# A recurrent-memory attention kernel with a dense branch: two more dense tiles put off into the steps, another layout of what is put off, and K's first matmul set moved into Q's group

## The chip, the cores and the metric

The kernel runs on one core of one Trainium2 chip. The metric is the device time of one execution in microseconds (us). Its engines here: PE (TensorE, matmuls; its weight loads are listed as PEld), DVE (VectorE), ACT (ScalarE), POOL (GpSimd) and SP (SyncE, which here only issues transfers). Each takes its instructions in the order in which the program gives them.

## The reference

Two branches read the same x (2048 tokens of 512), and a gate mixes them. Branch A goes over the tokens in 64 segments of 32. Each segment is put behind a memory of 8 rows, all 40 rows go through a 32-head attention, and the first 8 rows of its output are the memory of the next segment: the 64 steps must be done one after the other. Branch B is a layer norm and a two-layer network with GELU, and has no such chain.

```python
g = _sigmoid((x * gate_w).sum(-1, keepdims=True))
# branch A, for s in range(64), mem = mem0 at first
h = concatenate([mem, x[:, 32*s:32*s+32]], axis=1)          # 40 rows
q, k, v = (einsum('btd,dhe->bhte', h, W) for W in (Wq, Wk, Wv))
p = softmax(where(mask, einsum('bhqe,bhke->bhqk', q, k) * scale, -1e9))
o = einsum('bhte,hed->btd', einsum('bhqk,bhke->bhqe', p, v), Wo)
mem = o[:, :8];  outs.append(o[:, 8:])
# branch B
b = gelu(layernorm(x) @ w1 + b1) @ w2 + b2                  # 512 -> 1376 -> 512
return g * a + (1 - g) * b
```

## The kernel before

All instructions are in an order written out by hand, and each engine keeps to it.

**The front.** Branch B comes first, while the weights of branch A are loaded. It goes over 8 blocks of two tiles of 128 tokens. For each block there are 11 units, one for each 128 rows of the hidden layer: `a_mm` makes four matmuls of 256 columns (first layer, both tiles) and a Gelu on ACT into `hTm`; two units later `b_mm` makes one matmul of 512 columns for each tile of the block that is not in `DEF` (second layer, L487), and `ct_out` evicts the finished tile and stores it in DRAM (`c_dr`). The tiles in `DEF`, (1, 3, 5, 9, 11, 13, 15), are put off: `spill` (L501) stores their hidden layer in DRAM (`h_dr`) on SP's queue, 6 units in one transfer and 5 in a second. SP's queue also has the loads of x (`ld_x`), of the weights Wv, Wq, Wk, Wo (`loads`, L320 and L323, in this order) and the transposed loads `load_xT` (L102), all in program order. After the blocks come two `b_mm` that are left and `first()`, which makes the first tile's left-over Q, K and V.

**The hand-off.** The steps' tiles take memory that the front used. POOL clears the two `UT` tiles there (L615) once the front's users are through, and then copies into `QT` (`prep_q`, L249), which the first step's scores need.

**The steps.** Four steps, si = 0 to 3, share one tile of 128 tokens; `T` is the tile's number. A step holds 8 memory rows and 24 of its 32 tokens; the other 8 tokens of the four steps are done together, as fill, a tile ahead or behind (`side`, `run`). PE's order in a step: Q and K in four groups of four `qk_unit` (one for each chunk kc of the 512 inputs; each is four matmuls of 512 columns, side by side in the array's columns, called a set below), then scores, V, the sums for the softmax, attention times V (`av`), the output projection (`wo_pass`, eight sets), and `new_mem`, which makes the next memory, transposed, in three parts: ACT casts `w` (L741), PE gathers rows with `SelM` (L750), and DVE copies them into chunk 0, chunk 1 and chunks 2 and 3 of the next step's `hT` (L752). The next step's first `qk_unit` needs chunk 0, its second chunk 1, and so on.

**The put-off tiles in the steps.** `mlp` yields half sets: four matmuls of 256 columns into bank `W` (L678), 22 for a tile, and after the last of a tile `mlp_out` (L669) evicts W on DVE and stores the tile. From step 1 on a step has two such slots, `next(mlp, None)`, one ahead of `msum(1)` and one ahead of `recip_x`; tile 0's step si = 2 and the last tile's first steps have more. `recip_x` loads as many hidden-layer pieces `hm` as were used up (`hm_load`), between the store of R and the load of Rb on SP's queue.

**Banks.** The accumulators are U[0] to U[3], X1, X2, SbF and W. The four Q and K groups go to U[0] to U[3] in order; `out_sel` of tile T - 2 uses U[2] at si = 0, ahead of new_mem, which uses U[0], U[1] and a part of SbF.

Of the kernel before, what the change touches and what calls it, by code (L numbers as in the profile page):

```python
# [10 lines left out]
BF16 = mybir.dt.bfloat16  # L11
I32 = mybir.dt.int32
ACTF = mybir.ActivationFunctionType
ALU = mybir.AluOpType
# [14 lines left out]
def kernel(ctx, tc, A_x, A_mem0, A_Wq, A_Wk, A_Wv, A_Wo, A_seg_len, B_x, B_w1, B_b1, B_w2, B_b2, gate_w, out):  # L29
    nc = tc.nc  # L30
    P = 128
    _, S, Dm = A_x.shape
    H, Dh = A_Wq.shape[1], A_Wq.shape[2]
    M = A_mem0.shape[1]
# [4 lines left out]
    KC = Dm // P  # L39
    NT = S // P  # L40
    SPT = P // seg
    FC = (F + P - 1) // P
# [9 lines left out]
    scale = float(Dh) ** -0.5  # L52
# [5 lines left out]
    dram = ctx.enter_context(tc.tile_pool(name="dram", bufs=1, space=DRAM))  # L58
# [6 lines left out]
    omg = pers.tile([P, NT], FP32)  # L65
    w2_sb = pers.tile([P, FC, Dm], BF16)
    c_dr = dram.tile([S, Dm], BF16, name="c_dr")
    DEF = (1, 3, 5, 9, 11, 13, 15)
    h_dr = {T: dram.tile([FC, P, P], BF16, name=f"h_dr{T}") for T in DEF}
    r_dr = [dram.tile([P, NG], FP32, name=f"r_dr{i}") for i in range(2)]  # L70


# [17 lines left out]
    FR = F - (FC - 1) * P  # L90
# [20 lines left out]
    U = [lps.tile([P, 512], FP32, name=f"U{i}") for i in range(4)]  # L111
# [13 lines left out]
    def qk_unit(bk, G, t, hf, kc):  # L125
        h0, h1 = HF[hf]
        for j in range(4):
            nc.tensor.matmul(bk[32 * j:32 * j + 32, :], lhsT=G[:, kc, :], rhs=W5[t][:, kc, h0:h1, j, :],  # L128
                             start=(kc == 0), stop=(kc == KC - 1), tile_position=(0, 32 * j))
# [171 lines left out]
    with tc.tile_pool(name="mlpw", bufs=1) as mlpw, \  # L301
         tc.tile_pool(name="mwork", bufs=2) as mwork, \
         tc.tile_pool(name="msmall", bufs=2) as msmall:
        TB = 2
# [103 lines left out]


        for i in range(2):  # L410
            nc.gpsimd.memset(hTm[i][FR:P, FC - 1, :], 1.0)
        z_all = mlpw.tile([P, NT], FP32)
        th = mlpw.tile([P, NT], FP32)

# [57 lines left out]
        def bp(blk, tt):  # L472
            return U[2 * (blk % 2) + tt]

        def a_mm(blk, fc):
            rows = min(P, F - fc * P)
            n = blk * FC + fc
            hp = (SbF, W, U[3], SbF)[n] if n < 4 else (W, SbF)[n % 2]
            for kc in range(KC):
                nc.tensor.matmul(hp[:rows, 0:TB * P], lhsT=w1_sb[:, kc, fc * P:fc * P + rows], rhs=yTs[blk][:, kc, :], start=(kc == 0), stop=(kc == KC - 1))  # L480
            nc.scalar.activation(out=hTm[blk % 2][:rows, fc, :], in_=hp[:rows, 0:TB * P], func=ACTF.Gelu_apprx_tanh, bias=b1_sb[:rows, fc:fc + 1], scale=1.0)

        def b_mm(blk, fc):
            rows = min(P, F - fc * P + 1)
            tts = [tt for tt in range(TB) if blk * TB + tt not in DEF]
            for tt in tts:
                nc.tensor.matmul(bp(blk, tt)[:], lhsT=hTm[blk % 2][:rows, fc, tt * P:(tt + 1) * P],  # L487
                                 rhs=w2_sb[:rows, fc, :], start=(fc == 0), stop=(fc == FC - 1))
            if fc == FC - 1:
                for tt in tts:  # L490
                    if tt == 0 or blk == NBLK - 1:
                        ct_out(blk, tt)
                    else:
                        late.append(lambda: ct_out(blk, 1))

        def spill(blk, a, b):
            for tt in range(TB):
                T = blk * TB + tt
                if T in DEF:
                    src = hTm[blk % 2][:, :, tt * P:(tt + 1) * P]  # L500
                    nc.sync.dma_start(h_dr[T][a:b].rearrange("f p t -> p f t"), src[:, a:b])  # L501

        late = []

        def ct_out(blk, tt):
            T = blk * TB + tt
            ct = mwork.tile([P, Dm], BF16, tag="ct", bufs=4, name="ct")
            if blk < NBLK - 1:
                nc.scalar.activation(out=ct[:], in_=bp(blk, tt)[:], func=ACTF.Copy, scale=omg[:, T:T + 1])
            else:  # L510
                nc.vector.tensor_scalar(out=ct[:], in0=bp(blk, tt)[:], scalar1=omg[:, T:T + 1], scalar2=None, op0=ALU.mult)
            (nc.gpsimd if blk < NBLK - 1 else nc.sync).dma_start(c_dr[T * P:(T + 1) * P, :], ct[:])

        def first_h():
            m0p = X1[:].bitcast(BF16)[:, 0:KC * M].rearrange("p (k m) -> p k m", k=KC)
# [31 lines left out]
        for n, (blk, fc) in enumerate(units):  # L547
            a_mm(blk, fc)
            if n == len(units) - 1:
                dummy = msmall.tile([P, 1], FP32, tag="dummy", name="dummy")  # L550
                nc.scalar.activation(out=dummy[:], in_=omg[:, 0:1], func=ACTF.Exp)
            while late:
                late.pop(0)()
            if n >= LAG:
                b_mm(*units[n - LAG])
            if fc == 0:
                if blk >= 1:
                    gates(blk - 1)
                if blk + 1 < NBLK:
                    prep(blk + 1)  # L560
                else:
                    gate_sums(blk)
                    for _ in consts():
                        pass
            if blk + 1 < NBLK:
# [58 lines left out]
    def run(n):  # L624
        for _ in range(n):
            next(fill, None)
# [25 lines left out]
    def hm_load(n):  # L652
        for _ in range(n):
            if work:
                T, fc = work.pop(0)
                hm = cw.tile([P, P], BF16, tag="hm", bufs=5, name="hm")
                nc.sync.dma_start(hm[:], h_dr[T][fc])
                hms.append((T, fc, hm, 1))

    def hm_load4():  # L660
        x = cw.tile([P, Dm], BF16, tag="c", name="c").rearrange("p (k t) -> p k t", k=KC)
        T, fc = work[0]
        nc.sync.dma_start(x[:], h_dr[T][fc:fc + KC].rearrange("f p t -> p f t"))
        for k in range(KC):
            hms.append((*work.pop(0), x[:, k], 0))

# [74 lines left out]
            nc.scalar.copy(out=w[:, a:b], in_=bk[:, a:b])  # L741
        return w

    def new_mem(w, hn, n):

        k0, nk = ((0, 1), (1, 1), (2, 2))[n]
        bk = (U[0][:, 0:M], U[1][:, 0:M], xs8z)[n]
        for k in range(nk):
            for c in range(4):
                nc.tensor.matmul(bk[32 * c:32 * c + 32, M * k:M * k + M], lhsT=w[:, (k0 + k) * P + 32 * c:(k0 + k) * P + 32 * c + 32], rhs=SelM[:],  # L750
                                 start=n < 2, stop=True, skip_group_check=True, tile_position=(0, 32 * c))
        nc.vector.tensor_copy(out=hn[:, k0:k0 + nk, RIDE:32], in_=bk.rearrange("p (k m) -> p k m", k=nk))  # L752


    WS = ((2, 2, 1), (2, 2, 2), (2, 2, 2), (2, 2, 2))
    for s in range(nseg):
        T, si = divmod(s, SPT)
# [16 lines left out]
            load_xT(T + 2)  # L774
        if s in (2, (NT - 1) * SPT):
            hm_load4()
        for n, (t, hf) in enumerate(((0, 0), (1, 0), (0, 1), (1, 1))):
            bk = U[n]
            for kc in range(KC):
                qk_unit(bk, hc, t, hf, kc)  # L780
            if n == 0:
                flush(act_q, 9)
                flush(dve_q, 9)
            qk_tr(qk_cast(bk[:]), (QT, KT)[t], hf, LEFT * (1 - t))
            if n == 0:
                mask_put(1)
# [68 lines left out]
        new_mem(w, hn, 1)  # L855
        run(1)
        new_mem(w, hn, 2)
        for _ in fill:
            pass
        if si == 3 and T + 2 < NT:  # L860
# [197 lines left out]
```

## Time and profile before

| | us |
|---|---|
| median of 3 runs | 759.55 |
| lowest and highest | 757.79, 761.52 |
| the profiled execution | 759.91 |
| its span | 758.1 |
| busy: PE, ACT, DVE, POOL | 741.6, 537.3, 398.5, 274.8 |
| TensorE clock granted, mean | 0.999 |

The span is from the first to the last instruction of the profiled execution; its own time has some 1.8 us around it. Busy times are unions, so that matmuls that overlap count once. A matmul's record has a modelled end, with a tail behind its streaming: what a set costs is read from the distance of starts.

### The profile page before, as it was taken

What the parts mean: (1) busy time and instruction counts of PE and PEld (TensorE: products, weight loads), DVE (VectorE), ACT (ScalarE), POOL (GpSimd) and SP (SyncE); (2) the same over time, 40 slices, a digit from 0 to 9 for tenths busy, and PEclk for the clock granted to TensorE, in tenths of its full rate; (3) what the DMA queues carried; (4) which work ended last, traced back from release to release, by engine and by line L of the source; (5) the groups of instructions that cost most, each with busy time, mean ns of one, the idle gap of its engine ahead of it and who ended that gap; (6) DMA issues with size and microseconds to landing.
All of it is one profiled execution on the core that took longest, in us unless ns stands there. A gap on an engine that the chain in (4) does not pass through costs nothing.

```text
span 758.1 us, 45047 instructions
## 1 busy us (share of the span) xinstructions
PE 741.6 (98%) x19742; PEld 423.4 (56%) x19742; DVE 398.5 (53%) x1414; ACT 537.3 (71%) x1628; POOL 274.8 (36%) x517
## 2 busy tenths in 40 slices
PE   8999999999999999999999999999999999999997
PEld 5776455555555555555555556555555555555554
DVE  5767544545455545446454545445454545455454
ACT  5667677777777777777777777776777777677764
POOL 4001234433344343344333443434443344333441
PEclk9999999999999999999999999999999999999999
DMA  9999523222222323222222213231222212222222
GB/s 294 333 309 334 154 74 63 68 85 77 72 66 67 91 67 94 66 82 60 82 78 75 85 36 99 67 83 57 76 77 84 82 56 74 66 87 70 62 81 61
DMA packets 74971, 75.70 MB, mean 100 GB/s; under 512 B 42505, under 2 KB 64882, under 8 KB 73234
## 3 DMA queue, kind: packets, MB, share of 16 engines
q1 hardware_dynamic: 73730, 71.07, 30.7%
q8 instruction: 156, 2.56, 1.4%
q0 software_dynamic: 496, 1.18, 0.7%
q10 hardware_dynamic: 544, 0.52, 0.2%
q14 instruction: 45, 0.37, 0.2%
HBM read 59.49 MB, written 6.98 MB: 88 GB/s over the span
## 4 chain that ended last, share of the span: by engine, by line
PE 86%; issue 1%; ACT 0%; DVE 0%; DMA 0%; POOL 0%; DVEq 0%
PE U L128 33%; PE X L159 18%; PE X L147 17%; PE X L128 4%; PE U L290 3%; PE W L678 2%; PE U L147 2%; PE U L266 1%; PE U L750 1%; PE SbF L266 1%; PE SbF L705 1%; PE U L295 1%; PE U L277 1%; PE U L280 0%; PE U L270 0%
## 5 line engine op out<-in xcount | busy, mean ns | idle before, releaser
L734 POOL TENSOR_TENSOR UT<-XR,Rb 128x384 bf16<-128x384 bf16 x126 | 140.3, 1136 | 309.0 <-DMA Rb<-r_dr 237.8
L133 ACT CAST Tb<-U 128x512 bf16<-128x512 f32 x288 | 168.7, 586 | 81.8 <-PE U L128 78.9
L128 PEld LDWEIGHTS <-hT 128*32 128x32 bf16 x4096 | 107.6, 96 | 100.5 <-DVE hT L752 8.1
L147 PE MATMUL X<-Wv_sb,hT 128*32 128x512 bf16 x2048 | 144.6, 378 | 0.3 <-issue 0.2
L128 PE MATMUL U<-Wq_sb,hT 128*32 128x512 bf16 x2048 | 136.5, 381 | 0.2 <-DVE hT L752 0.2
L128 PE MATMUL U<-Wk_sb,hT 128*32 128x512 bf16 x2048 | 133.1, 379 | 0.0
L159 PE MATMUL X<-Wo_sb,UT 128*32 128x512 bf16 x2016 | 121.1, 380 | 0.0
L752 DVE CAST hT<-U 128x8 bf16<-128x8 f32 x126 | 20.9, 166 | 166.1 <-PE U L750 126.0
L812 ACT CAST V<-X 128x256 bf16<-128x256 f32 x256 | 88.7, 372 | 15.9 <-PE X L147 3.3
L137 DVE STREAM_TRANSPOSE QT<-Tb 128x256 f32<-128x256 f32 x128 | 56.6, 442 | 73.3 <-ACT Tb L133 72.5
L159 PEld LDWEIGHTS <-UT 128*32 128x32 bf16 x2048 | 56.4, 96 | 54.8 <-issue 14.3
L711 ACT CAST XR<-U 128x256 bf16<-128x256 f32 x252 | 78.5, 436 | 0.0
L741 ACT CAST w<-X 128x128 bf16<-128x128 f32 x189 | 44.8, 310 | 44.9 <-PE X L159 44.9
L137 DVE STREAM_TRANSPOSE KT<-Tb 128x256 f32<-128x256 f32 x128 | 57.0, 445 | 30.9 <-ACT Tb L133 23.2
L734 POOL TENSOR_TENSOR UL<-XR,Rb 128x128 bf16<-128x128 bf16 x126 | 60.3, 502 | 0.0
L147 PEld LDWEIGHTS <-hT 128*32 128x32 bf16 x2048 | 47.2, 94 | 21.6 <-issue 1.2
L726 POOL TENSOR_TENSOR racc<-racc,R 128x72 f32<-128x72 f32 x63 | 21.2, 336 | 93.6 <-DVE R L724 66.7
L843 ACT CAST UT<-U 128x64 bf16<-128x64 f32 x252 | 35.8, 226 | 26.4 <-PE U L295 26.2
L795 ACT ACTIVATE E<-U 128x64 bf16<-128x64 f32 (+1 forms) x128 | 35.0, 273 | 11.7 <-PE U L270 11.2
L480 PEld LDWEIGHTS <-w_sb 128*128 128x128 bf16 (+1 forms) x352 | 33.5, 100 | 15.1 <-issue 2.4
L750 PEld LDWEIGHTS <-w 128*32 128x32 bf16 x1008 | 23.6, 93 | 32.0 <-ACT w L741 25.2
L159 PE MATMUL X<-Wo_sb,UL 128*32 128x512 bf16 x512 | 39.4, 379 | 0.3 <-issue 0.3
(179 smaller groups left out, 1237.5 us busy)
## 6 DMA issues: line engine op xcount, KB each, us to landing
Rb<-r_dr SPq DMA_DIRECT2D x63, 512.0 KB, 4.0
Wv_sb<-in_A_Wv_dram SPq DMA_DIRECT2D x4, 1024.0 KB, 7.1
Wq_sb<-in_A_Wq_dram SPq DMA_DIRECT2D x4, 1024.0 KB, 8.7
Wk_sb<-in_A_Wk_dram SPq DMA_DIRECT2D x4, 1024.0 KB, 8.8
Wo_sb<-in_A_Wo_dram SPq DMA_DIRECT2D x4, 1024.0 KB, 11.3
VP<-VL SPq DMA_DIRECT2D x64, 64.0 KB, 3.5
hm<-h_dr SPq DMA_DIRECT2D x69, 32.0 KB, 2.1
c<-c_dr SPq DMA_DIRECT2D x16, 128.0 KB, 3.2
```

Source lines behind the costliest of these rows:

```text
L128: nc.tensor.matmul(bk[32 * j:32 * j + 32, :], lhsT=G[:, kc, :], rhs=W5[t][:, kc, h0:h1, j, :], start=(kc == 0), stop=(kc == KC - 1), tile_ ...
L133: nc.scalar.copy(out=Tb[:], in_=bk.rearrange("p (a b e) -> p a e b", a=8, b=2))
L137: nc.vector.transpose(out=dst[:, 8 * hf:8 * hf + 8, c0:c0 + 32, :].rearrange("p a r b -> p a (r b)").bitcast(FP32), in_=Tb[:].rearrange("p ...
L147: nc.tensor.matmul(bk[32 * j:32 * j + 32, :], lhsT=G[:, kc, :], rhs=Wv5[:, kc, 4 * vb:4 * vb + 4, j, :], start=(kc == 0), stop=(kc == KC - ...
L159: nc.tensor.matmul(bk[32 * c:32 * c + 32, :], lhsT=U_[:, j, i, :], rhs=Wo_sb[:, 4 * i + j, :], start=(n == 0), stop=(n == NW - 1), tile_po ...
L480: nc.tensor.matmul(hp[:rows, 0:TB * P], lhsT=w1_sb[:, kc, fc * P:fc * P + rows], rhs=yTs[blk][:, kc, :], start=(kc == 0), stop=(kc == KC - 1))
L711: nc.scalar.copy(out=XR[:, j], in_=U[j][:, 0:NG * 40].rearrange("p (i q) -> p i q", q=40)[:, :, 0:32])
L734: nc.gpsimd.tensor_tensor(out=out[:, :, 4 * h:4 * h + 4, o:o + b - a], in0=XR[:, :, 4 * h:4 * h + 4, a:b], in1=Rb[:, h, :, :, a:b], op=ALU ...
L741: nc.scalar.copy(out=w[:, a:b], in_=bk[:, a:b])
L795: nc.scalar.activation(out=E[:, 4 * i2:4 * i2 + 4, c], in_=Sb[i2][:, :, c], func=ACTF.Exp, scale=scale)
L812: nc.scalar.copy(out=V[:, i0:i0 + 2, :].rearrange("p i e -> p (i e)"), in_=(X1, X2)[vb][:, 256 * h:256 * h + 256])
L843: nc.scalar.copy(out=UT[s % 2][:, j, :, 0:M], in_=U[j][:, 0:NG * 40].rearrange("p (i q) -> p i q", q=40)[:, :, 32:40])
```

## The change

It has four parts. (1) Tiles 7 and 14 are put off too, which makes nine put-off tiles; block 7 then has no second layer in the front, its first layer takes turns over four banks instead of two, and the `b_mm` behind the blocks, the late evictions and their second path go. (2) `hTm` and `h_dr` are laid out so that a partition's units of one tile lie together: a spill writes 1536 or 1280 bytes in one piece for each partition instead of six or five pieces of 256. (3) A third slot for a half set stands in the steps with si > 0, after `run(W3)`, ahead of new_mem. (4) K's set for kc = 0 is issued right after Q's set for kc = 0; K's first group goes to U[2] and Q's second to U[1]; out_sel goes to U[1], and new_mem's second part to U[2] where si = 0.

```diff
-    DEF = (1, 3, 5, 9, 11, 13, 15)
-    h_dr = {T: dram.tile([FC, P, P], BF16, name=f"h_dr{T}") for T in DEF}
+    DEF = (1, 3, 5, 7, 9, 11, 13, 14, 15)
+    h_dr = {T: dram.tile([P, FC, P], BF16, name=f"h_dr{T}") for T in DEF}
...
-        hTm = [mlpw.tile([P, FC, TB * P], BF16, name=f"hTm{i}") for i in range(2)]
+        hTm = [mlpw.tile([P, TB, FC, P], BF16, name=f"hTm{i}") for i in range(2)]
...
-            hp = (SbF, W, U[3], SbF)[n] if n < 4 else (W, SbF)[n % 2]
+            hp = (SbF, W, U[3], SbF)[n] if n < 4 else (W, SbF, U[2], U[3])[n % 4] if blk == NBLK - 1 else (W, SbF)[n % 2]
...
-            nc.scalar.activation(out=hTm[blk % 2][:rows, fc, :], in_=hp[:rows, 0:TB * P], func=ACTF.Gelu_apprx_tanh, bias=b1_sb[:rows, fc:fc + 1], scale=1.0)
+            nc.scalar.activation(out=hTm[blk % 2][:rows, :, fc, :], in_=hp[:rows, 0:TB * P].rearrange("p (t c) -> p t c", t=TB), func=ACTF.Gelu_apprx_tanh, bias=b1_sb[:rows, fc:fc + 1], scale=1.0)
...
                 for tt in tts:
-                    if tt == 0 or blk == NBLK - 1:
-                        ct_out(blk, tt)
-                    else:
-                        late.append(lambda: ct_out(blk, 1))
+                    ct_out(blk, tt)
...
-                    src = hTm[blk % 2][:, :, tt * P:(tt + 1) * P]
-                    nc.sync.dma_start(h_dr[T][a:b].rearrange("f p t -> p f t"), src[:, a:b])
+                    nc.sync.dma_start(h_dr[T][:, a:b], hTm[blk % 2][:, tt, a:b])
...
-                f0 = 8 if (blk + 1) * TB - 1 in DEF else 7 if blk == 0 else 6
+                f0 = 8
...
-            if n == 1:
-                for m in range(len(units) - LAG, len(units)):
-                    b_mm(*units[m])
...
-            return out_sel(T - 2, U[2])
+            return out_sel(T - 2, U[1])
...
-                nc.sync.dma_start(hm[:], h_dr[T][fc])
+                nc.sync.dma_start(hm[:], h_dr[T][:, fc])
...
-        bk = (U[0][:, 0:M], U[1][:, 0:M], xs8z)[n]
+        bk = (U[0][:, 0:M], U[1 if si else 2][:, 0:M], xs8z)[n]
...
-        for n, (t, hf) in enumerate(((0, 0), (1, 0), (0, 1), (1, 1))):
-            bk = U[n]
-            for kc in range(KC):
+        for n, (t, hf) in enumerate(QK4):
+            bk = U[(0, 2, 1, 3)[n]]
+            for kc in range(n == 1, KC):
                 qk_unit(bk, hc, t, hf, kc)
+                if n == kc == 0:
+                    qk_unit(U[2], hc, *QK4[1], 0)
...
         run(W3)
+        if si:
+            next(mlp, None)
         for _ in extra(T, si):
             pass
-        new_mem(w, hn, 0)
+        new_mem(w, hn, 0, si)
```

More of the change, by code (lines that the diff above doesn't have):

```diff
@@ L410 @@
         for i in range(2):
-            nc.gpsimd.memset(hTm[i][FR:P, FC - 1, :], 1.0)
+            nc.gpsimd.memset(hTm[i][FR:P, :, FC - 1, :], 1.0)
         z_all = mlpw.tile([P, NT], FP32)
@@ L486, in b_mm @@
             for tt in tts:
-                nc.tensor.matmul(bp(blk, tt)[:], lhsT=hTm[blk % 2][:rows, fc, tt * P:(tt + 1) * P],
+                nc.tensor.matmul(bp(blk, tt)[:], lhsT=hTm[blk % 2][:rows, tt, fc, :],
                                  rhs=w2_sb[:rows, fc, :], start=(fc == 0), stop=(fc == FC - 1))
@@ L499, in spill @@
                 if T in DEF:
-                    src = hTm[blk % 2][:, :, tt * P:(tt + 1) * P]
-                    nc.sync.dma_start(h_dr[T][a:b].rearrange("f p t -> p f t"), src[:, a:b])
-        late = []
+                    nc.sync.dma_start(h_dr[T][:, a:b], hTm[blk % 2][:, tt, a:b])
         def ct_out(blk, tt):
@@ L507, in ct_out @@
             ct = mwork.tile([P, Dm], BF16, tag="ct", bufs=4, name="ct")
[L508 to L512, printed above, removed]
+            nc.scalar.activation(out=ct[:], in_=bp(blk, tt)[:], func=ACTF.Copy, scale=omg[:, T:T + 1])
+            nc.gpsimd.dma_start(c_dr[T * P:(T + 1) * P, :], ct[:])
         def first_h():
@@ L551 @@
                 nc.scalar.activation(out=dummy[:], in_=omg[:, 0:1], func=ACTF.Exp)
-            while late:
-                late.pop(0)()
             if n >= LAG:
@@ L662, in hm_load4 @@
         T, fc = work[0]
-        nc.sync.dma_start(x[:], h_dr[T][fc:fc + KC].rearrange("f p t -> p f t"))
+        nc.sync.dma_start(x[:], h_dr[T][:, fc:fc + KC])
         for k in range(KC):
@@ L742, in wo_pass, with new_mem @@
         return w
-    def new_mem(w, hn, n):
+    def new_mem(w, hn, n, si):
         k0, nk = ((0, 1), (1, 1), (2, 2))[n]
-        bk = (U[0][:, 0:M], U[1][:, 0:M], xs8z)[n]
+        bk = (U[0][:, 0:M], U[1 if si else 2][:, 0:M], xs8z)[n]
         for k in range(nk):
@@ L752, in new_mem @@
         nc.vector.tensor_copy(out=hn[:, k0:k0 + nk, RIDE:32], in_=bk.rearrange("p (k m) -> p k m", k=nk))
+    QK4 = ((0, 0), (1, 0), (0, 1), (1, 1))
     WS = ((2, 2, 1), (2, 2, 2), (2, 2, 2), (2, 2, 2))
@@ L850 @@
         run(W3)
+        if si:
+            next(mlp, None)
         for _ in extra(T, si):
             pass
-        new_mem(w, hn, 0)
+        new_mem(w, hn, 0, si)
         run(1)
-        new_mem(w, hn, 1)
+        new_mem(w, hn, 1, si)
         run(1)
-        new_mem(w, hn, 2)
+        new_mem(w, hn, 2, si)
         for _ in fill:
```

## The prediction

> **What bounds the kernel now.** I read the page first: its busy rows, then its slices.
>
> ```profile
> span 758.1 us, 45047 instructions
> PE 741.6 (98%) x19742; PEld 423.4 (56%) x19742; DVE 398.5 (53%) x1414; ACT 537.3 (71%) x1628; POOL 274.8 (36%) x517
> ```
>
> TensorE is busy 98% of the span, so nearly every matmul set counts, unless it lies in a hole. The holes are small, and the timeline of one step's end (step 31 into 32) shows where they are. The columns are start, length, engine, line, and in brackets the idle time before and what ended it.
>
> ```profile
> 402.01 0.61 PE L159 MATMUL X<-Wo_sb,UL 128*32 128x512 bf16 x8
> 402.24 0.71 ACT L741 CAST w<-X 128x128 bf16<-128x128 f32 x3 [0.74 <-PE X L159]
> 402.56 0.10 PEld L750 LDWEIGHTS <-w 128*32 128x32 bf16 x4 [0.43 <-ACT w L741]
> 402.56 0.19 PE L750 MATMUL U<-SelM,w 128*32 128x8 bf16 x4
> ...
> 402.87 0.44 DVE L752 CAST hT<-U 128x8 bf16<-128x8 f32 x2 [2.55 <-PE U L750]
> ...
> 403.05 0.20 PE L750 MATMUL SbF<-SelM,w 128*32 128x8 bf16 x8
> ...
> 403.10 1.11 PE L128 MATMUL U<-Wq_sb,hT 128*32 128x512 bf16 x16
> ...
> 403.36 2.95 PEld L128 LDWEIGHTS <-hT 128*32 128x32 bf16 x60 [0.17 <-DVE hT L752]
> 403.37 0.17 DVE L752 CAST hT<-SbF 128x16 bf16<-128x16 f32 x1
> ...
> 404.04 1.04 PE L128 MATMUL U<-Wk_sb,hT 128*32 128x512 bf16 x16
> ...
> 404.90 1.04 PE L128 MATMUL U<-Wq_sb,hT 128*32 128x512 bf16 x16
> ```
>
> An undisturbed group of 16 takes 404.90 - 404.04 = 0.86 us from its start to the next one's; so four column matmuls of 512 columns (a set) cost 0.215 us, whatever the record's tail adds. Two holes follow. The two fill sets that start at 402.01 have streamed out at 402.44, and the next matmul, new_mem's first, starts at 402.56, when ACT's first w cast is there: 0.12 us. Then the first Q group takes 404.04 - 403.10 = 0.94 us, 0.08 more than an undisturbed one, because its second set waits for the second copy into hT on DVE, and its third for the copy at 403.37. How often, the waits tell:
>
> ```profile
> PEld L750 <- ACT w L741: 25.2, 65, 0.9
> PEld L128 <- DVE hT L752: 8.1, 47, 0.4
> ```
>
> The second row has 47 waits: all steps but those after si = 0, where one more fill set stands at the end.
>
> **The change, part by part.** Sums are made against the profiled execution (759.91 us with a span of 758.1) and carried over, as a difference, to the median, 759.55.
>
> *K's first set inside the first Q group.* No set is added; K's kc 0 fills the 0.08 us hole. 47 x 0.08 = **-3.8 us**. The Q group ends 0.215 - 0.08 us later for its cast, K's does not; ACT is idle there, so I cost this and the exchanged banks at nothing (bounds: 0, and 0.1 us in each of 63 steps if the cast order did matter).
>
> *The front.* Tile 7 is the second column of block 3, tile 14 the only one of block 7 that was not put off. Their 22 second-layer matmuls go. The rows of PE in block 3 and block 7 give the price:
>
> ```profile
> 35.51 0.60 PE L480 MATMUL SbF<-yT,w_sb 128*128 128x256 bf16 x4
> 35.95 0.59 PE L487 MATMUL U<-w_sb,hTm 128*128 128x512 bf16 x2
> 36.38 0.60 PE L480 MATMUL W<-yT,w_sb 128*128 128x256 bf16 x4
> ...
> 72.53 0.60 PE L480 MATMUL SbF<-yT,w_sb 128*128 128x256 bf16 x4
> 72.97 0.38 PE L487 MATMUL U<-w_sb,hTm 128*128 128x512 bf16 x1
> 73.19 0.60 PE L480 MATMUL W<-yT,w_sb 128*128 128x256 bf16 x4
> ```
>
> A unit takes 0.87 us with two of them and 0.66 with one: 0.215 each, 22 x 0.215 = 4.7 us less PE work before the first step. But PE does not set the moment of the hand-off:
>
> ```profile
> 70.00:80.00 10.00, 10.00 (x126) 5.69 (x129) 5.20 (x32) 7.46 (x16) 0.35 (x1) 1.00 1.09 354
> ...
> 79.39 1.40 SPq L188 DMA_DIRECT2D VP<-VL  x1
> ...
> 82.92 1.42 POOL L615 MEMSET UT<- 128x768 bf16 x2 [12.57 <-DMA VP<-VL]
> 84.28 0.41 POOL L249 COPY QT<-QL 128x128 f32<-128x128 f32 x1
> ...
> 84.74 0.28 PE L266 MATMUL SbF<-QT,KT 128*32 128x40 bf16 x16 [0.68 <-POOL QT L249]
> ```
>
> The DMA share (next to last column) is 1.09: the queue is full to the end. UT's memset, whose memory was the front's, waits for the last transfers of the front; the copy into QT stands behind it on POOL; and the first scores waited 0.68 us for that copy. So PE, 4.7 us earlier, would be at the first scores at 84.74 - 0.68 - 4.7 = 79.4, and would wait for the DMA. What becomes of the DMA's end? First the pieces, two windows (last columns: share, GB/s), the second when most packets are the spills' 256 bytes:
>
> ```profile
> 76.00:78.00 2.00, 2.00 (x34) 0.66 (x26) 0.75 (x1) 1.47 (x4) 0.00 (x0) 1.00 1.10 367
> 80.00:81.00 1.00, 1.00 (x24) 0.53 (x20) 0.64 (x2) 0.72 (x2) 0.00 (x0) 1.00 0.87 204
> ```
>
> At full share that is 367 / 1.10 = 334 GB/s against 204 / 0.87 = 234. A spilled tile is 192 + 160 KB, 360 KB in decimal: 1.54 us in small pieces, 1.08 in the new ones of 1280 and 1536 bytes, taking these to move like the first window's.
>
> ```profile
> h_dr<-hTm SPq DMA_DIRECT2D x7, 192.0 KB, 4.3
> h_dr<-hTm SPq DMA_DIRECT2D x7, 160.0 KB, 6.8
> ```
>
> All in all 7 x 1.54 = 10.8 us of spills become 9 x 1.08 = 9.7, and tile 7's own store (131 KB, 0.4 us) goes: 1.5 us less. The Trainium skill ("DMA: Bandwidth & Descriptors", Specifications) sets line rate at pieces of 512 bytes or more and has smaller ones rewritten. Read as half rate, that would save 7 x 2.16 - 9.7 + 0.4 = 5.8 us, and the hand-off would be PE's again; the windows have 0.70 of the rate, not half.
>
> Against it stands a move on SP's queue. Tile 7's first spill is new, and it is issued ahead of the two transposes of x and the second pair of Wq loads:
>
> ```profile
> 21.24 0.38 SPq L501 DMA_DIRECT2D h_dr<-hTm  x1
> ...
> 29.26 0.38 SPq L501 DMA_DIRECT2D h_dr<-hTm  x1
> ...
> 34.49 4.84 SPq L102 DMA_TRANSPOSE xT<-in_A_x_dram  x2
> ...
> 39.90 1.49 SPq L320 DMA_DIRECT2D Wq_sb<-in_A_Wq_dram  x2
> ```
>
> The first spills of blocks 1 and 2 are 8.0 us apart, so block 3's cannot go before 37.3: its Gelus are not done. The transposes then start 3 us later than 34.49, and so may the loads behind them, with the queue drained meanwhile. Bounds of the hand-off: 4.7 + 0.68 = 5.4 us earlier (PE alone sets it) and 1.5 us later (3 - 1.5). I take **-1.2 us**: the smaller load, less a little of that delay, as the earlier spills' savings let the queue empty sooner.
>
> *The third half set.* 22 x 2 = 44 half sets move into the steps, and fit into the 0.12 us hole before new_mem where si > 0. Their price:
>
> ```profile
> L678 PE MATMUL W<-w_sb,hm 128*32 128x256 bf16 x552 | 38.2, 272 | 0.0
> L669 DVE TENSOR_SCALAR ct<-W,omg 128x512 bf16<-128x512 f32 x7 | 5.3, 750 | 0.3
> ```
>
> 256 columns stream in half of 0.215, 0.108 us: from 402.44 to 402.55, with w there at 402.56. That is cover with nothing to spare; counting the slots, 45 are used. At 0.02 us each **+0.9 us**; without cover 45 x 0.108 = 4.9. SP gets about half a load of hm more in each step, between the store of R and the load of Rb; those wait for the store's landing anyhow, so nothing.
>
> *Where the tiles end.* This is the term I would not leave out. A tile has 22 half sets, and four steps now hold 2 + 3 + 3 + 3 = 11, so the last half of a tile always falls on the same slot. Counted through, it is the new one: at si = 2 of steps 10, 18, 26, 34, 42, 50 and 58 (tiles 3 to 14), where before it was the slot ahead of recip_x. The instruction order of the changed kernel has it so: DVE's eviction of W, the 750 ns row above, stands directly in front of the three copies into hT, in order. The half set ends 402.44 + 0.27 = 402.71, DVE follows a matmul 0.12 us later (402.75 to 402.87), evicts until 403.58, and only then makes the first copy, 0.17 us, done at 403.75 instead of 403.04. PE's next Q set, there at 403.10, waits for it: 0.65 us. Behind DVE's eviction are queued the three hT copies; PE waits for the first and has nothing else. 7 x 0.65 = 4.6, and tile 1, which ends between the second and third copy of step 2, some 0.4: **+5.0 us**. (0 if DVE were done earlier.) The Trainium skill ("PSUM — Partial Sum Buffer", Engine vs sequencer instructions) calls VectorE's queue strictly first in, first out; by that rule the copies cannot pass the eviction. If they could, this term would be nothing.
>
> Sum: -3.8 - 1.2 + 0.9 + 5.0 = +0.9, 760.8 us for the profiled execution, **760.5 us** on the median: no change that shows. A measurement of this kernel tells about 0.5%, 3.8 us, from no change.
>
> **The rivals.**
>
> *The hand-off comes with PE.* If the DMA queue empties early enough, the front gives 5.4 instead of 1.2 us: 4.2 less, 756.3 us. For it: fewer, larger pieces, and everything from block 4 on is issued 2.4 us sooner. Against it: share 1.09 to the end.
>
> *The clock falls at the hand-off.* PE would stand from 79.4 to 83.5. The kernel's first matmuls show a slow clock after idling:
>
> ```profile
> 1.47 4.57 PE L533 MATMUL U<-ident 128*128 128x512 bf16 x11 [1.47 <-POOL ident masks.py:199]
> ```
>
> Eleven of 512 columns in 4.57 us, some 0.4 us each instead of 0.215. As long a stretch at half speed in step 0 costs 4.57 / 2 = 2.3 us: 762.8. Against it: a hole of 4 us may be too short. The Trainium skill ("TensorE: Matmul & The Clock Gate", Part 1) halves the clock after one idle window of about 3.4 us; by that rule it falls here.
>
> *The new half set is not covered* (slower). Place: the slot before new_mem, 45 times. If w is there before the half set has streamed, it pushes everything behind it by up to 0.108 us: 4.9 instead of 0.9, 764.5. It decides from where w is ready 0.1 us sooner, or the half set starts 0.1 us later; for it, the 0.01 us margin; against it, w's wait ended 65 of 65 times on ACT.
>
> *The eviction is hidden.* If DVE starts it before new_mem's matmuls are out and overlaps the rest, 5.0 goes: 755.5. Against it: 750 ns against a hole of 0.4.
>
> **How the numbers follow.** Chances: forecast 0.45, PE-timed hand-off 0.15, clock 0.15, uncovered half set 0.15, hidden eviction 0.10. Faster than 755.75 are most of the last and under half of the first rival, and a little of the forecast: 0.17. Slower than 763.35 are most of the uncovered case, half of the clock's and some of the forecast, whose terms can add up: 0.26. Between: 0.57. The range goes from the hidden eviction less 1 us to the uncovered case plus 1.5, since the runs of the kernel before alone differ by 3.7: 754.5 to 766.
>
> **What would show it.** Right: the first Q group 1.07 us or so with K's set in it and its wait on hT gone; a wait of PE on DVE's hT copies of some 0.65 us in seven steps, eight apart; first scores after 82.5 us with PE idle some 4 us before them, ended by POOL's QT; new_mem's start unmoved against Wo's last set. Wrong: the first scores near 79.5 (the DMA was no bound), no such waits in steps 10 to 58, or steps with si > 0 longer by 0.1 us throughout.

## The result, and the profile after

| | before | after |
|---|---|---|
| median of 20 runs each, side by side, us | 760.03 | 764.08 |
| lowest and highest | 757.79, 761.81 | 758.94, 768.26 |
| the profiled execution, and its span | 759.91, 758.1 | 763.07, 761.2 |

The ratio of after to before is 1.0049 (95% interval 1.0034 to 1.0064), and the medians lie 4.05 us apart: slower, by about the least that can be told from no change. The forecast was +0.95 us.

The page's first lines, of after:

```profile
span 761.2 us, 45395 instructions
...
PE 736.4 (97%) x19888; PEld 431.9 (57%) x19896; DVE 396.6 (52%) x1415; ACT 535.6 (70%) x1627; POOL 274.5 (36%) x516
```

PE is busy 5.2 us less, in a span that is 3.1 us longer, so it stands idle 8.3 us longer than before. Four places of the timeline of after say where. First, a step's end with nothing special in it (step 31 into 32, as shown of before):

```profile
415.95 0.30 PE L664 MATMUL W<-w_sb,hm 128*32 128x256 bf16 x4
...
416.07 0.19 PE L736 MATMUL U<-SelM,w 128*32 128x8 bf16 x4
...
416.42 0.39 DVE L738 CAST hT<-U 128x8 bf16<-128x8 f32 x2 [2.51 <-PE U L736]
...
416.64 0.40 PE L128 MATMUL U<-Wq_sb,hT 128*32 128x512 bf16 x4
416.87 0.39 PE L128 MATMUL U<-Wk_sb,hT 128*32 128x512 bf16 x4
416.88 0.17 DVE L738 CAST hT<-SbF 128x16 bf16<-128x16 f32 x1
417.08 0.82 PE L128 MATMUL U<-Wq_sb,hT 128*32 128x512 bf16 x12
417.73 0.82 PE L128 MATMUL U<-Wk_sb,hT 128*32 128x512 bf16 x12
418.38 0.60 PE L128 MATMUL U<-Wq_sb,hT 128*32 128x512 bf16 x8
```

K's first set stands between Q's first and second; both first groups together take 418.38 - 416.64 = 1.74 us, against 404.90 - 403.10 = 1.80 before. The new half set (415.95) streams in the 0.12 us before new_mem's first matmul.

Second, the end of step 10, the first of the seven in which a put-off tile ends in the new slot:

```profile
194.67 0.29 PE L664 MATMUL W<-w_sb,hm 128*32 128x256 bf16 x4
...
194.79 0.19 PE L736 MATMUL U<-SelM,w 128*32 128x8 bf16 x4
...
195.01 0.75 DVE L655 TENSOR_SCALAR ct<-W,omg 128x512 bf16<-128x512 f32 x1 [2.38 <-PE U L736]
...
195.68 0.23 DVE L738 CAST hT<-U 128x8 bf16<-128x8 f32 x2
...
195.89 0.40 PE L128 MATMUL U<-Wq_sb,hT 128*32 128x512 bf16 x4 [0.41 <-DVE hT L738]
```

From new_mem's first matmul to Q it is 195.89 - 194.79 = 1.10 us, where step 31 has 416.64 - 416.07 = 0.57: DVE evicts W for 0.75 us before it makes the copies into hT, and PE stands. The waits of after (engine, tile, releaser: us in total, times, longest) count it:

```profile
DVE ct L655 <- PE U L736: 17.6, 7, 3.0
...
PEld L736 <- ACT w L727: 15.2, 63, 0.9
...
PEld L128 <- DVE hT L738: 5.3, 12, 0.7
```

Seven evictions by the first row, and the last row has 12 waits with up to 0.7 us each, where before had 47 short ones. The middle row, PE's wait for ACT's w ahead of new_mem, has lost 10 us in total and still ends on ACT all 63 times: the half sets went into that wait.

Third, the hand-off, with slices of the span behind it (last three columns: granted PE clock, DMA share, GB/s):

```profile
77.60 1.04 PE L128 MATMUL U<-Wk_sb,hT 128*32 128x512 bf16 x16
80.51 1.42 POOL L601 MEMSET UT<- 128x768 bf16 x2 [12.71 <-DMA VP<-VL]
81.87 0.41 POOL L249 COPY QT<-QL 128x128 f32<-128x128 f32 x1
82.33 0.28 PE L266 MATMUL SbF<-QT,KT 128*32 128x40 bf16 x16 [3.69 <-DMA hm<-h_dr]
...
82.46 1.96 PE L147 MATMUL X<-Wv_sb,hT 128*32 128x512 bf16 x20
```

```profile
82.00:83.00 1.00, 0.67 (x32) 0.47 (x35) 0.06 (x1) 0.23 (x1) 1.00 (x4) 0.94 0.29 65
83.00:84.00 1.00, 1.00 (x16) 0.47 (x12) 0.00 (x0) 0.12 (x1) 0.10 (x1) 0.50 0.24 71
84.00:85.00 1.00, 1.00 (x48) 0.57 (x41) 0.35 (x1) 0.59 (x3) 0.00 (x0) 0.50 0.59 125
85.00:86.00 1.00, 1.00 (x24) 0.57 (x20) 0.56 (x3) 0.48 (x3) 0.00 (x0) 0.50 0.09 23
```

The first scores come 2.4 us sooner (84.74 to 82.33), behind POOL's memset and copy as before (the bracket names a transfer, but the copy into QT ends at 82.28). PE stood for 3.69 us, and the clock granted to it is then 0.50 for some 3.4 us, from 82.9 to 86.3. From the scores to step 1's first Q set it takes 8.18 us instead of 6.95, so that step 1 starts 1.18 us sooner, not 2.4.

Fourth, the end. At the end of its program PE branches past code that is there as a fallback. The branch's length in before and in after (min, median, max in ns):

```profile
L941 PEldq COMPARE_BRANCH  x1: 1674/1674/1674, 755.0 to 755.0; - x1
```

```profile
L932 PEldq COMPARE_BRANCH  x1: 3685/3685/3685, 756.4 to 756.4; - x1
```

2.0 us more, in a place where the change did nothing. Two executions can be compared step by step if the stray holes of a step are kept apart from its length. As the length I take the mean of the four shortest steps of each si (10.51, 10.16, 10.21, 10.23 us before; 10.47, 10.17, 10.17, 10.17 after). Summed over steps 1 to 62, the two profiled executions compare so: start of step 1 -1.2, steps -2.1, evictions +4.3 (seven times 0.56, and 0.40 behind step 2), other holes of the steps +0.4, from step 63 on +1.7; together +3.1, the difference of the spans.

### The profile page after: what moved, and what is told of

It reads as the page before. It is cut to its first block, busy times and chain, and to the rows that moved or that the text cites. A ratio compares the mean times of both kernels' runs of the same rounds, so it can differ in the third digit from the quotient of the medians.

```text
span 761.2 us, 45395 instructions
## 1 busy us (share of the span) xinstructions
PE 736.4 (97%) x19888; PEld 431.9 (57%) x19896; DVE 396.6 (52%) x1415; ACT 535.6 (70%) x1627; POOL 274.5 (36%) x516
## 3 DMA queue, kind: packets, MB, share of 16 engines
q0 software_dynamic: 448, 1.05, 0.4%
## 4 chain that ended last, share of the span: by engine, by line
PE 89%; DMA 4%; DVE 3%; issue 2%; ACT 2%; SPq 1%; DVEq 0%; ACTq 0%
PE U L128 32%; PE X L159 19%; PE X L147 16%; PE X L128 4%; PE U L290 3%; PE W L664 3%; PE U L147 2%; PE U L266 1%; DMA w_sb<-in_B_w_dram 1%; DMA xt<-in_A_x_dram 1%; PE SbF L480 1%; PE W L480 1%; PE SbF L266 1%; DVE junk L463 1%; DMA h_dr<-hTm 1%
## 5 line engine op out<-in xcount | busy, mean ns | idle before, releaser
L128 PEld LDWEIGHTS <-hT 128*32 128x32 bf16 x4096 | 109.9, 96 | 98.5 <-DVE hT L738 5.3
L128 PE MATMUL U<-Wq_sb,hT 128*32 128x512 bf16 x2048 | 145.3, 380 | 3.1 <-DVE hT L738 3.1
L128 PE MATMUL U<-Wk_sb,hT 128*32 128x512 bf16 x2048 | 144.8, 379 | 0.0
L159 PE MATMUL X<-Wo_sb,UT 128*32 128x512 bf16 x2016 | 122.7, 380 | 1.6 <-issue 1.4
L147 PEld LDWEIGHTS <-hT 128*32 128x32 bf16 x2048 | 47.9, 95 | 20.5 <-issue 0.2
L664 PE MATMUL W<-w_sb,hm 128*32 128x256 bf16 x728 | 51.7, 273 | 0.0
```

The costliest lines, as they stand in the source:

```text
L159: nc.tensor.matmul(bk[32 * c:32 * c + 32, :], lhsT=U_[:, j, i, :], rhs=Wo_sb[:, 4 * i + j, :], start=(n == 0), stop=(n == NW - 1), tile_po ...
L664: nc.tensor.matmul(W[32 * c:32 * c + 32, cc], lhsT=hm[:, 32 * c:32 * c + 32], rhs=w2_sb[:, fc, cc], start=(fc == 0 and h == 0), stop=(fc = ...
```

## The experiments

Each ran beside the kernel before on the same chip, and the ratio is to that. The kernel before had a median of 757.71 us beside the first four, 756.86 beside the next four, 757.99 beside the three after those and 757.24 beside the last, so the medians of different groups are not to be compared with each other. A ratio can differ from the quotient of its medians by one per mille, which is 0.76 us.

| kernel | median, us | ratio, 95% interval |
|---|---|---|
| after, eviction late | 757.39 | 0.9996 (0.9970 to 1.0022) |
| after, kept warm | 758.56 | 1.0019 (0.9992 to 1.0047) |
| before + interleave | 755.70 | 0.9980 (0.9958 to 1.0003) |
| before + layout | 756.66 | 0.9982 (0.9952 to 1.0013) |
| before + interleave + layout | 753.12 | 0.9959 (0.9934 to 0.9983) |
| after, eviction late and kept warm | 752.99 | 0.9954 (0.9934 to 0.9975) |
| after, again | 760.01 | 1.0049 (1.0025 to 1.0073) |
| before, again | 757.76 | 1.0013 (0.9990 to 1.0035) |
| after, short matmuls | 760.84 | 1.0044 (1.0031 to 1.0057) |
| after, hint earlier | 763.66 | 1.0085 (1.0059 to 1.0111) |
| before + interleave + layout, hint earlier | 754.48 | 0.9960 (0.9940 to 0.9980) |
| before + the two tiles put off | 766.92 | 1.0130 (1.0099 to 1.0161) |

**The eviction behind new_mem's copies.** `mlp_out` is noted down and done after new_mem's third part.

```diff
                     if fc == FC - 1:
-                        mlp_out(T)
+                        due.append(T)
...
         new_mem(w, hn, 2, si)
+        pay()
```

> The changed kernel, with DVE's eviction of W put behind the three copies into hT where a tile ends in the third slot (it was in front of them). Theory: in seven steps PE waits 0.56 us for DVE before the next step's first Q set, in one (step 3) 0.40 us, and this takes all of that away: 4.3 us less than the changed kernel's 764.1, so 759.8, and the distance from new_mem's first matmul to the next Q set is 0.55 us in steps 11, 19, ... 59 as in the others, where it was 1.10. Rival: the loss is not the eviction but holes in PE's instruction supply, which the 176 matmuls more in the steps make worse: then the seven waits go but other holes stay, and the time stays above 763.

The timeline of this kernel at the same place:

```profile
195.34 0.19 PE L744 MATMUL U<-SelM,w 128*32 128x8 bf16 x4
...
195.69 0.40 DVE L746 CAST hT<-U 128x8 bf16<-128x8 f32 x2 [2.68 <-PE U L744]
...
195.91 0.40 PE L128 MATMUL U<-Wq_sb,hT 128*32 128x512 bf16 x4
...
196.24 0.74 DVE L655 TENSOR_SCALAR ct<-W,omg 128x512 bf16<-128x512 f32 x1
```

0.57 us from new_mem to Q, the eviction beside Q. No step has the long distance any more, and 1.0049 - 0.9996 = 0.0053 is 4.0 us, with intervals that do not overlap. The eviction's place costs about what the trace says, 4.3.

**PE kept warm.** 17 matmuls of 512 columns into W between K and the first scores.

```diff
+        if s == 0:
+            for _ in range(17):
+                nc.tensor.matmul(W[:, 0:512].rearrange("p (a b) -> p a b", a=4), lhsT=ident[:], rhs=ident[:].unsqueeze(1).to_broadcast([P, 4, P]), start=True, stop=True, skip_group_check=True)
         scores(s, 0)
```

> The changed kernel, with 17 matmuls of 512 columns into the unused bank W between the first step's K and its scores, where PE stood idle for 3.7 us. They compute nothing that is used. Theory: the idle stretch made the clock fall, and the first step ran 20 V matmul sets in 1.96 us instead of 1.25; with PE kept busy the first scores stay where they were, at 82.3 us, the first step is 1.2 us shorter, and the time is 762.9. Rival: the first step is slow because its data come late, not because of the clock: no change, 764.1.

```profile
78.59 3.84 PE L796 MATMUL W<-ident 128*128 128x512 bf16 x17
80.44 1.42 POOL L601 MEMSET UT<- 128x768 bf16 x2 [12.61 <-DMA VP<-VL]
82.36 0.28 PE L266 MATMUL SbF<-QT,KT 128*32 128x40 bf16 x16
82.51 1.25 PE L147 MATMUL X<-Wv_sb,hT 128*32 128x512 bf16 x20
```

The first scores are where they were (82.36), the twenty V matmuls take 1.25 us instead of 1.96, and step 1 starts at 89.67 instead of 90.51. So the fallen clock cost 0.84 us in this pair of executions. The runs gained 2.3 us against after, but the two intervals overlap, so the 1.2 us expected is neither shown nor refuted by them. In this trace the branch at the end was short too, 543 ns.

**The interleave alone**, with the banks that go with it, in the kernel before.

```diff
-            bk = U[n]
-            for kc in range(KC):
+            bk = U[(0, 2, 1, 3)[n]]
+            for kc in range(n == 1, KC):
                 qk_unit(bk, hc, t, hf, kc)
+                if n == kc == 0:
+                    qk_unit(U[2], hc, *QK4[1], 0)
```

> The kernel before, with only K's first set moved inside the first Q group and the banks exchanged. Theory: 0.064 us less in each of the 46 steps that waited for DVE's copies into hT, as the changed kernel's trace has it: 2.9 us, 757.1. Rival: the wait only moves to the next set or to the scores: 760.0.

```profile
194.91 0.39 PE L128 MATMUL U<-Wq_sb,hT 128*32 128x512 bf16 x4
...
195.13 0.39 PE L128 MATMUL U<-Wk_sb,hT 128*32 128x512 bf16 x4
...
195.34 0.82 PE L128 MATMUL U<-Wq_sb,hT 128*32 128x512 bf16 x12
195.99 0.82 PE L128 MATMUL U<-Wk_sb,hT 128*32 128x512 bf16 x12
...
196.64 1.03 PE L128 MATMUL U<-Wq_sb,hT 128*32 128x512 bf16 x16
```

The sets are 0.215 us apart, undisturbed. Both first groups take 196.64 - 194.91 = 1.73 us here (1.724 in the median) against 1.80 in before, in the 46 steps that had the hole; over all steps their times add up to 3.4 us less. The shortest steps are 10.45, 10.16, 10.15 and 10.16 us: 2.9 us less over 62 steps; si = 1 had no hole to fill and gains nothing. The runs gained 1.5 us, in an interval that reaches from 3.2 to nothing. Against these steps, after's are 0.8 us longer in sum: that is the third half set beside the interleave, forecast at 0.9.

**The layout alone**, in the kernel before.

```diff
-    h_dr = {T: dram.tile([FC, P, P], BF16, name=f"h_dr{T}") for T in DEF}
+    h_dr = {T: dram.tile([P, FC, P], BF16, name=f"h_dr{T}") for T in DEF}
...
-        hTm = [mlpw.tile([P, FC, TB * P], BF16, name=f"hTm{i}") for i in range(2)]
+        hTm = [mlpw.tile([P, TB, FC, P], BF16, name=f"hTm{i}") for i in range(2)]
```

> The kernel before, with only the spilled tiles' layout changed (1536 and 1280 bytes in one piece instead of 256). Theory: seven tiles save some 0.5 us of transfer time each, so UT's memset comes 1.5 to 2.5 us earlier than 82.9 us; PE waited only 0.68 us there, so the time falls by 0.7 us to 759.3, and no more. Rival: the transfers' end is set by the weights, whose order and size are the same: the memset stays within 0.5 us of 82.9 and the time at 760.0.

```profile
80.76 1.42 POOL L614 MEMSET UT<- 128x768 bf16 x2 [11.30 <-DMA VP<-VL]
...
82.99 0.27 PE L266 MATMUL SbF<-QT,KT 128*32 128x40 bf16 x16
83.12 1.25 PE L147 MATMUL X<-Wv_sb,hT 128*32 128x512 bf16 x20
```

The memset comes 2.2 us sooner than before's 82.92, nearly all that it does in after, and the scores no longer wait for POOL: here PE sets the hand-off, and with a warm clock step 1 starts at 89.93, sooner than in after. That is 1.8 us sooner than in before, where 0.7 was expected, because PE itself came about 1 us sooner to the scores. Executions differ by as much: step 1 starts at 90.93 and 90.56 in the two other traces with this layout and seven tiles, and at 91.25 to 91.69 in the three traces with the old one. The runs' gain of 1.4 us cannot be told from 0.7, nor from none.

**Interleave and layout together**, without the two tiles, and **after with both cures**, the late eviction and the warm PE.

> The kernel before with the interleaved K set and with the spilled tiles stored by partition; no tile more is put off and no third half set is added. Theory (the parts add up, and the two tiles put off bring only the queue of evictions in front of the copies): the interleave's 46 x 0.065 plus shorter steps, measured as -2.0 us alone, and the hand-off's -1.05 alone, together -2.5 to -4 us against the kernel before (ratio 0.995 to 0.997); first scores at 82.5 to 83.0, step 1 from 89.5 to 90.0, UT's memset at 80.3 to 81.0, and no distance of 1.1 us between new_mem and the next Q. Rival (the two gains are the same time counted twice, or are lost in the gaps of PE's instruction supply): within 1 us of the kernel with the interleave alone, -1 to -2 us.

> The changed kernel with the put-off tile's eviction behind new_mem's copies, and with 17 matmuls between K and the first scores that keep PE busy there. Theory (the eviction costs 4.3 us and the fallen clock 0.8 to 1.2): -5 us against the changed kernel, -1 to -2 us against the kernel before, ratio 0.997 to 0.999; step 1 from 89.5 to 89.9; no distance of 1.1 us between new_mem and Q. By the theory that putting two tiles more off is worth nothing at the hand-off it is not faster than the kernel with interleave and layout alone. Rival (the two tiles put off do pay once their eviction is out of the way): 1 us or more below that kernel.

Two versions with the same time: 0.9959 and 0.9954. The first is the sum of its parts (0.9980 and 0.9982); the second lies 0.0095, 7.2 us, under after, near the sum of its two cures (0.0053 + 0.0030), where 5 us were expected. They are the fastest measured, and they differ by the two tiles and what goes with them: once the eviction and the idle stretch are cured, putting off two more tiles brings nothing that can be measured, as the theory said. With these intervals, a gain or a loss of 2 us would not show. In the first, step 1 came at 90.93, later than expected, since its memset came at 81.81.

**The same two kernels again**, to see what of a trace belongs to the code.

> The changed kernel once more, unaltered, for a second trace on the chip that runs the others. Theory: 4 us (3 to 5) above the kernel before; seven distances of 1.1 us between new_mem and Q, first scores at 82.3, step 1 at 90.5 as in the first trace. The branch at the end: if its length (3.7 us in the first trace) hangs on the code, it comes out at 3.4 to 4.0 us again; rival, if it hangs on the execution, anywhere from 0.5 to 4 us.

> The kernel before once more, unaltered: ratio 1 within 0.2%. The branch at the end: 1.5 to 1.9 us if its length hangs on the code, anywhere from 0.5 to 4 us if it hangs on the execution. The gaps of PE's instruction supply over the 62 steps: 10 to 13 us as in the first trace if they belong to the code, off by 2 us or more if they belong to the execution.

After's seven stalls come again; its first scores came at 83.81 and step 1 at 91.83, while before's step 1 came at 91.25. In this pair the hand-off lost 0.6 us where the first pair gained 1.2: its sign hangs on the execution. In the four traces with after's hand-off (after twice, eviction late, hint earlier) step 1 starts between 90.51 and 91.83, on average 0.15 us sooner than in the three with before's (91.25 to 91.69). The branch took 4.05 us in after and 1.45 in before, close to the first traces, so the code has a hand in it. The holes strewn over the steps (what a step has over the length taken for its si) were 7.7 us in before, 11.8 in its first trace. In all 14 traces they make 7 to 13 us, without the evictions, in no order that follows the changes.

**Short matmuls instead of the long ones**, to part the clock from the branch: 17 of 8 columns.

```diff
-                nc.tensor.matmul(W[:, 0:512].rearrange("p (a b) -> p a b", a=4), lhsT=ident[:], rhs=ident[:].unsqueeze(1).to_broadcast([P, 4, P]), start=True, stop=True, skip_group_check=True)
+                nc.tensor.matmul(W[:, 0:8], lhsT=ident[:], rhs=ident[:, 0:8], start=True, stop=True, skip_group_check=True)
```

> The changed kernel with the same 17 matmuls as the kernel kept warm, at the same place and into the same bank, but of 8 columns instead of 512: as many instructions on PE, hardly any work (17 x 0.03 = 0.5 us inside a wait of 3.7). It tells apart the two things that the 17 long ones did, the clock and the branch. Theory (clock by the idle stretch, branch by where PE's program stands when its next block of code is asked for): the clock falls again in step 0, first scores at 82.3 to 83.8 and step 1 from 8.0 to 8.2 us behind them, as in the changed kernel (8.18 and 8.02) and not 6.9 to 7.3; the branch comes out at 0.5 to 0.9 us as with the long ones; together -2.5 to -3.3 us against the changed kernel (ratio to the kernel before 1.000 to 1.002). Rival (what shortened the branch was the warm clock or the calmer start, not the place in the program): branch 3.5 to 4.1 us, and the time that of the changed kernel, ratio 1.004 to 1.005.

```profile
78.33 0.58 PE L796 MATMUL W<-ident 128*128 128x8 bf16 x17
...
81.75 0.28 PE L266 MATMUL SbF<-QT,KT 128*32 128x40 bf16 x16 [2.83 <-DMA hm<-h_dr]
...
81.88 1.61 PE L147 MATMUL X<-Wv_sb,hT 128*32 128x512 bf16 x20
```

```profile
L935 PEldq COMPARE_BRANCH  x1: 638/638/638, 755.4 to 755.4; - x1
```

Half came out: the clock fell (0.50 for 3.4 us; scores to step 1: 8.08 us) and the branch was short, both as the theory had it. But the time did not follow: 1.0044, 0.4 us under after, not 2.5 to 3.3. What the branch's length in one profiled execution is worth in the median of many is therefore not shown.

**The hint earlier.** The program gives a hint that the branch will be taken, so that the code at its target can be fetched ahead. This hint now stands in front of the last av stage, 120 PE instructions sooner, once in after and once in the kernel with interleave and layout.

```diff
     nc.vector.tensor_reduce(out=tot[:, 2:3], in_=R[:, nx], axis=AX.X, op=ALU.min)
+    tc.no_sync_barrier()
+    tc.mark_branch_hint_location("general", "LikelyTaken", engines=[mybir.EngineType.PE])
     av(s, V, E)
...
     flush(act_q, 9)
-    tc.no_sync_barrier()
-    tc.mark_branch_hint_location("general", "LikelyTaken", engines=[mybir.EngineType.PE])
```

> The changed kernel with the hint that has the branch's target fetched ahead put 120 PE instructions earlier, in front of the last step's av stage instead of behind it (about 3 us earlier); nothing else differs. Theory (the branch waits for a block of code that is asked for only 1.04 us after the branch has been reached): the block is asked for before the branch, which then takes 0.5 to 1.7 us instead of 3.7 to 4.0; -2 to -3.3 us against the changed kernel, ratio to the kernel before 1.000 to 1.002. Rival (the block is asked for when PE's stream of code has room, whatever the hint): branch 3.5 to 4.1 us, ratio 1.004 to 1.005.

> The kernel with the interleave and the layout alone, with the hint put earlier in the same way. Theory: its branch (3.5 us) falls to 0.5 to 1.7 us, and it is the fastest of all, -2 to -3 us against the kernel without the earlier hint, ratio to the kernel before 0.992 to 0.994. Rival (the hint's place decides nothing): 0.995 to 0.997 as without it, branch 3.4 to 4.0 us.

The branches, of after with the hint earlier and of the other:

```profile
L932 PEldq COMPARE_BRANCH  x1: 3965/3965/3965, 752.3 to 752.3; - x1
```

```profile
L943 PEldq COMPARE_BRANCH  x1: 396/396/396, 749.7 to 749.7; - x1
```

One long as without it, one short, and the short one did not show in the time: it left the ratio at 0.9960 (0.9959 without). The long one stands at 1.0085, above after's 1.0049, with intervals that just overlap. Its profiled execution, at 759.19 us the fastest of its six, shows nothing slower than the two of after. Whether and why the others were slower stays open. What the traces do show is when the code is fetched: PE's program arrives in transfers of 16 KB, and with branches of 0.5 to 1.7 us the last one ahead of it started 1.2 to 1.9 us before the branch was reached (five traces), or already 4.4 us before (the short one here); with the interleave alone it started 0.2 us before, and the branch took 2.8; with those of 3.5 to 4.3 us the next one started 1.03 to 1.06 us after (seven traces). In these thirteen traces, the short one here left out, the branch ended 1.3 to 1.6 us after that transfer did. The distance looks like a matter of where the branch stands in the program: the start is 1.04 or 1.05 us after in all five traces with as many matmuls as after, and 1.79 to 1.86 us before in all three with 17 more, long or short. What sets it in the others is open.

**The two tiles alone**, with the third slot that takes them, in the old layout and order.

```diff
-    DEF = (1, 3, 5, 9, 11, 13, 15)
+    DEF = (1, 3, 5, 7, 9, 11, 13, 14, 15)
...
         run(W3)
+        if si:
+            next(mlp, None)
```

> The third part of the change by itself: tiles 7 and 14 put off into the steps, with the third half set and the smaller first block's schedule that go with it, in the old layout of the spilled tiles and with the old order of K's first set. Theory (the parts add up: the whole is +4.05 us, the interleave alone -2.0, the layout alone -1.05, so this part is +7): ratio 1.008 to 1.010; seven distances of 1.1 us between new_mem and the next Q (4.3 us with step 3's), and a hand-off that brings nothing or less: PE arrives at the first scores at 78.5 to 79.5, stands idle for 4 to 6 us while the last pieces of 256 bytes land, first scores at 83 to 85.5, step 0 slower by 0.8 to 1.4 us for the fallen clock, step 1 from 91.5 to 93.5. Rival (putting two tiles off pays at the hand-off, and only the eviction takes it back): first scores at 81 to 82.5, step 1 from 89 to 90.5, ratio 1.002 to 1.005.

```profile
84.35 1.42 POOL L602 MEMSET UT<- 128x768 bf16 x2 [14.57 <-DMA VP<-VL]
85.71 0.40 POOL L249 COPY QT<-QL 128x128 f32<-128x128 f32 x1
...
86.17 0.32 PE L266 MATMUL SbF<-QT,KT 128*32 128x40 bf16 x16 [5.56 <-DMA hm<-h_dr]
...
86.33 2.35 PE L147 MATMUL X<-Wv_sb,hT 128*32 128x512 bf16 x20
```

This is the worst part, +9.8 us, beyond the expected 7. PE comes to the scores at 80.6 and stands 5.56 us, since the transfers end later than before; the memset is 1.4 us late, the V matmuls run cold, step 1 starts at 94.18, 2.5 us later than before, and the seven stalls follow. Against after, the layout is what pulls the hand-off forward: step 1 starts 2.4 to 3.7 us sooner with it here, more than the 1.3 to 1.8 us that it brought alone. That there are more spills to speed up would explain it; no run tests that. So the parts need not add up: by the ratios, interleave, layout and two tiles alone make -1.5 - 1.4 + 9.8 = +6.9 us and the whole 3.7, though the intervals are wide enough to hold that gap. The steps show another overlap: with the third half set and no interleave the shortest steps are no longer than before's (0.8 us less in sum, where traces with before's steps differ by 0.6). So the half set alone is covered, and beside it the interleave gains 1.2 us by the steps' lengths, where alone it gained 2.9.

## Why the prediction was right or wrong

*The eviction* (+5.0): right in place, count and cause, and confirmed by moving it. It measured 4.3 (0.56 each instead of 0.65, and 0.40 behind step 2 as named). The copies stand behind it in DVE's order, as the rule cited from the Trainium skill ("PSUM — Partial Sum Buffer", Engine vs sequencer instructions) has it; the trace agrees, 195.01 then 195.68.

*K's first set* (-3.8): right mechanism, somewhat too large. With the interleave alone the hole gave 0.076 us in 46 steps, 3.4 us in the two groups, 2.9 by the steps' lengths and 1.5 by the runs. In after it gave 0.06 us a step, 1.74 against 1.80 for the two groups.

*The third half set* (+0.9): 0.8, but not where I put it. The rival of the uncovered half set is out: new_mem's wait ended on ACT's w every time, and new_mem starts 0.31 us after the last other set in before and in after (medians, si > 0). The 0.8 us lie behind new_mem, mostly in the two first groups, which take 1.737 us in after and 1.724 with the interleave alone. So the size came out partly by luck.

*The hand-off* (-1.2): right sum in the first trace, by luck, from wrong parts. The DMA let the scores come 2.4 us sooner, twice what I took (82.33, just outside my sign of "after 82.5"); the fallen clock, which I kept as a rival at 2.3 us, took 1.2 of it back. The second trace made it +0.6. That step failed: I doubted that four microseconds of standing were enough, and they were, in all six traces where PE stood for 2.8 us or more. In the others it stood for at most 1.2 us there, and the clock stayed. The Trainium skill ("TensorE: Matmul & The Clock Gate", Part 1) gives one idle window of about 3.4 us; with 3.69 us of idling and a clock of 0.50, the trace agrees. The 2.83 us behind the short matmuls were enough too; together with these 0.58 us of hardly any work they make 3.4. My "the queue is full to the end" was read from a slice that ends at 80 us: between 80.5 and 82.5 the DMA share in before is 0.49 to 0.72. The term of the delayed transposes was mis-sized as well. SP's rows of after:

```profile
37.06 2.67 SPq L102 DMA_TRANSPOSE xT<-in_A_x_dram  x2
...
40.32 0.81 SPq L320 DMA_DIRECT2D Wq_sb<-in_A_Wq_dram  x2
```

They start 2.6 us later, near the 3 us forecast, but take 2.67 instead of 4.84 us, so that Wq behind them is only 0.4 us late.

*The hand-off with PE* (rival): out. PE waited 3.69 us for the end of the transfers and POOL behind it. The reading of the Trainium skill's 512 bytes ("DMA: Bandwidth & Descriptors", Specifications) as half rate would have made PE the bound. With the layout alone the memset came 2.2 us sooner; seven tiles would give 7 x 0.46 = 3.2 us at the 0.70 of before's windows and 7.6 at half rate, so 0.70 stands nearer.

*What no step had*: the end, +1.7 us in the first pair of traces, with the branch 2.0 longer. That pair's sum is +3.1 where I had +0.9: interleave +0.9 (2.9 instead of 3.8), evictions -0.7, half set -0.1, strewn holes +0.4, end +1.7, hand-off as said. The medians' 4.05 lies 0.9 above that sum, and the interval (2.6 to 4.9 us) holds it. Since a shorter branch did not shorten the runs, the end's part in the medians is not settled; the eviction's is.

## What to carry to other kernels

An instruction on an engine that is far from busy (DVE was busy for 53% of the span) can still cost most of its length when it stands in front of the one copy that the next step waits for: count through where the last piece of each unit falls, and put its eviction behind that copy. Work taken off an engine ahead of a hand-off that a transfer sets is not time won; it becomes standing, and here the standing cost the clock as well. Take a change apart before judging it: here two of its parts were worth 3 us together and the third cost more than that. But do not count on the parts to add up.

## What the runs showed of the hardware that was not expected

- Standing for 3.7 to 5.6 us in five traces, and for 2.8 us behind 0.58 us of short matmuls in a sixth, dropped PE's granted clock to 0.50, for 3.4 us in five of them and for 6.8 in the one with the eviction late. The V sets then ran 0.43 us apart, and step 0 took 0.8 to 1.2 us longer in after, and 1.9 in that one.
- A taken branch at the end of PE's program took 0.4 to 4.3 us in 14 traces; in all but the shortest it ended 1.3 to 1.6 us after the transfer of a 16 KB block of code. In two executions each it was 1.5 to 1.7 us in before and 3.7 to 4.1 in after.
- The same code had 7.7 and 11.8 us of strewn holes in its steps: 4.1 apart, as much as the whole change. One trace cannot show a part of 2 us by its span; the step lengths and the distances in it can.
